# A spectral filter and a GeGLU network with their gradients: the first group starts on four row tiles, tables and tails move

## The chip, the cores and the metric

The kernel runs on one NeuronCore of one Trainium2 chip. Times are device microseconds of one execution. TensorE is called PE here, VectorE DVE, ScalarE ACT, GpSimd POOL; SP only issues DMAs.

## What is computed

Two branches work on x (2048 x 576, bf16) and B_x of the same size, and a gate mixes them; the kernel returns the mixed output and the gradients of everything but B_x. The forward part of the reference, cut:

```python
g = sigmoid((x * gate_w).sum(-1, keepdims=True))
X = rfft2(x.astype(float32)) * (w_r + 1j * w_i)
a = irfft2(X, s=(2048, 576)).astype(bfloat16)
b = (gelu(x @ w_gate) * (x @ w_up)) @ w_down      # width of the hidden layer: 4608
out = g * a + (1 - g) * b
```

The network reads the same x in the kernel. Gradients follow from `grad_out` (dO): through the FFT branch (a second transform of g*dO), and through the network: dA = dO (1-g) w_down^T, the two hidden gradients dHg and dHu, three weight gradients and dx.

## The kernel before

**Layout.** The rows are held as 16 row tiles of 128. Each row tile is turned on PE (a matmul against the identity `ident`) into `xT` and `dOT`, whose five column chunks are the even and odd columns in two halves each and a tail of 64 columns, kept twice (partitions `LO` and `HI`). `titems` (L347) makes three items of a source's four row tiles: two of 1024 columns, one for the tails; each is a PSUM tile and a copy by DVE (`VC`) or ACT (`AC`).

**The first stage** runs `NG` = 18 groups of 256 hidden columns, in each 4 steps of four row tiles, 72 steps in all (`pr` in the loop at L944 to L1027). In a step `H_mm` (L378) multiplies z = dOT w_down^T (16 matmuls of 256 columns and four tail ones) into a PSUM tile of pool `pz` (one buffer), then xy = xT [w_gate, w_up] into two tiles of pool `ph` (two buffers): four tail matmuls, then 8 of 512 columns per tile (`full`). ACT scales z by 1 - g into `da` (`H_da`), and copies and squares xy (`H_act`); DVE does three operations in `H_ew1`; ACT does two sigmoids and DVE eight products in `H_ew2`, the last of which gives dHg. In group 0 the sigmoids and products of a step are held back until `da` of the next (`held`).

From group 1 on, the weight gradients of the group before follow the xy matmuls in a step, as units of two halves (`W_units`, L468): `u_dw` (16 matmuls a half), `u_dwd` (8 a half) and the tail (8 row tiles a half, two matmuls each, that use half of the array's columns). Their PSUM tiles are in pool `pw` (two buffers, opened at group 1 in the place of `pg`), and ACT copies them out.

**The transform units** are a list of 207 slots (`fft`, L890): `u1` and `u2` of the forward transforms (column and row part), `s2` and `s1` of the filter, `z`, `ztail` and `d` of the inverse ones, some empty (`gap`). Each takes a PSUM tile by `pftile` (L541), from group 1 on always from pool `pz`, the same buffer as z, and ACT copies it out. `want(pr)` (L910) says how many slots are done by step `pr`: `FIRST` for the first eight steps, then an even share. Of the n units of a step the first goes ahead of the last four xy matmuls (`xy_full(1, fft_next)`), the others go between the halves of W units, at the places that `spots` gives in estimated microseconds `at` of the W work so far (L1001 to L1009); what is left goes to the end of the step (L1010). Then come the stores and the step's sigmoids.

**Tables.** `build_D` makes column tables, `build_R` the row tables of four row tiles, `build_B` that of the filter; integer parts are made by DVE and POOL, the sines by ACT. The sines of `build_R` and `build_B` are put on the list `tb.late` and done by `run_late`. [...]

**The head** (L862 to L884): x of all row tiles and dO of the first eight are turned, the gate is computed for all rows (80 matmuls of one column), the column tables and half of the row tables are made; then step 0 begins. dO of the other eight is turned in step 0.

**The second stage** (from L1032) reads the stored hidden arrays back by transposing DMAs and multiplies out b and dx. The change doesn't touch it. The order on every engine is the order of the program.

Of the kernel before, what the change touches and what calls it, by code (L numbers as in the profile page):

```python
# [63 lines left out]
def iotas(nc, res, unit):  # L64
    tb = Tables()
    G = nc.gpsimd
    kw = dict(allow_small_or_imprecise_dtypes=True)
    tb.lrow = unit([HF], F32, name="lrow")
# [4 lines left out]
    G.iota(tb.dcol[:, 4:5], pattern=[[0, 1]], base=512, channel_multiplier=1, **kw)  # L73
    tb.dn = res.tile([P, 5], F32, name="dn")
    nc.vector.tensor_scalar(tb.dn[:], tb.dcol[:], 1.0 / D, None, op0=ALU.mult)
# [9 lines left out]
    tb.qcol_i = res.tile([P, 1], I32, name="qcol_i")  # L85
    G.iota(tb.qcol_i[:], pattern=[[0, 1]], base=0, channel_multiplier=1)
    par_i = res.tile([P, 1], I32, name="par_i")
    nc.vector.tensor_single_scalar(par_i[:], tb.qcol_i[:], 1, op=ALU.bitwise_and)
    tb.par = res.tile([P, 2], F32, name="par_f")
    nc.vector.tensor_copy(tb.par[:, 1:2], par_i[:])  # L90
    nc.vector.tensor_scalar(tb.par[:, 0:1], tb.par[:, 1:2], -1.0, 1.0, op0=ALU.mult, op1=ALU.add)
    nc.vector.tensor_scalar(tb.kadd[:, 0, 1:2], tb.par[:, 1:2], float(S // 2), float(S // 4), op0=ALU.mult, op1=ALU.add)
    tb.halfpi = res.tile([P, 1], F32, name="halfpi")
    nc.vector.memset(tb.halfpi[:], math.pi / 2)
    tb.pi = res.tile([P, 1], F32, name="pi")
    nc.vector.memset(tb.pi[:], math.pi * EPS_SCALE)
    tb.npi = res.tile([P, 1], F32, name="npi")
    nc.vector.memset(tb.npi[:], -math.pi * EPS_SCALE)
    tb.warm = res.tile([P, 1], F32, name="warm")
    nc.scalar.activation(tb.warm[:], tb.halfpi[:], ACT.Sin)  # L100
    tb.late = []
    tb.Dt = []
    return tb
# [7 lines left out]
def build_D(nc, tb, unit, res, c0, n):  # L111

    V = nc.vector
    step = 2.0 * math.pi / D
    TS = (nc.gpsimd if c0 else V).tensor_scalar
    X = unit([n, HF], F32, name="XD")
    y = unit([n, HF], F32, name="yD")  # L120
    for c in range(n):
        TS(y[:, c, :], tb.lrow[:], tb.dn[:, c0 + c:c0 + c + 1], MAGIC, op0=ALU.mult, op1=ALU.add)
    TS(y[:], y[:], -MAGIC, -float(D), op0=ALU.add, op1=ALU.mult)
    for c in range(n):
        V.scalar_tensor_tensor(X[:, c, :], tb.lrow[:], tb.dcol[:, c0 + c:c0 + c + 1], y[:, c, :],
                               op0=ALU.mult, op1=ALU.add)
    o = unit([n, 2, HF], name="Dt")
    V.scalar_tensor_tensor(y[:], X[:], -1.0, X[:], op0=ALU.mult, op1=ALU.max)
    nc.scalar.activation(o[:, :, 0, :], y[:], ACT.Sin, bias=tb.halfpi[:], scale=-step)
    nc.scalar.activation(o[:, :, 1, :], X[:], ACT.Sin, scale=-step * EPS_SCALE)  # L130
    if c0 < 4:
        tb.Dt += [o[:, c] for c in range(n)]
        return
    tails = unit([2, 2, HF], name="Dt")
    nc.gpsimd.memset(tails[HI, :, :, :], 0.0)
    for par in range(2):
        V.tensor_scalar(tails[LO, par], o[LO, 0], tb.par[LO, par:par + 1], None, op0=ALU.mult)
    tb.Dt += [tails[:, par] for par in range(2)]
# [90 lines left out]
def kernel(  # L229
# [32 lines left out]
    gwT = res.tile([P, 5], BF16, name="gwT")  # L262
    one = res.tile([1, 1], BF16, name="one")
    nc.vector.memset(one[:], 1.0)
    nc.vector.memset(gwT[:, 4:5], 0.0)
# [7 lines left out]
    def load_w(g, part):  # L273
# [4 lines left out]
        if part == 0:  # L278
            wgu = wts[g][0]
            for w, c0 in ((B_w_gate, 0), (B_w_up, FG)):  # L280
                cols = slice(c0, c0 + FG)
                LD.dma_start(wgu[:, 0:4, cols].rearrange("p (e k) f -> p e k f", e=2),
                             w[0:512, fsl].rearrange("(k p e) f -> p e k f", e=2, p=P))
                for r in (LO, HI):
                    LD.dma_start(wgu[r, 4, cols], w[512:D, fsl])
# [11 lines left out]
    ident = res.tile([P, P], BF16, name="ident")  # L297
    make_identity(nc, ident[:])
    tb = iotas(nc, res, unit)
# [5 lines left out]

    gwr = unit([D], name="gwr")
    LD.dma_start(gwr[0:1, :], gate_w.rearrange("(o d) -> o d", o=1))
    load_x(0)
    load_do(0)
    wdn = unit([2, D], name="wdn")  # L310
    LD.dma_start(wdn[:], B_w_down[0:FG, :].rearrange("(c p) d -> p c d", p=P))
    for k in range(1, 4):
        load_x(4 * k)
    load_do(4)
    load_w(0, 0)
    load_do(8)
    load_do(12)
# [9 lines left out]
    pg = pgs.enter_context(tc.tile_pool(name="pg", bufs=1, space=PSUM))  # L327
# [8 lines left out]
    tb.Rt = []  # L336
# [3 lines left out]
    hctr = [0]  # L340

    def headps():
        hctr[0] += 1
        pool, tag = ((pg, "pg"), (ph, "xy"), (pz, "z"), (ph, "xy"))[hctr[0] % 4]
        return pool, tag

    def titems(src, dst, t0, ps, copies, n=4):  # L347

        def item(k, cs):
            def f():  # L350
                tp_ = ps(BF16).rearrange("p b (j t m) -> p b j t m", j=2, t=4)
                for j, c in enumerate(cs):
                    for tt in range(n):
                        if c < 4:
                            nc.tensor.transpose(tp_[:, 0, j, tt, :], src[:, t0 + tt, eo(c)], ident[:])
                        else:
                            for r in (LO, HI):
                                nc.tensor.transpose(tp_[r, 0, 0, tt, :], src[:, t0 + tt, 512:D], ident[:])
                copies[k](dst[:, cs[0]:cs[0] + len(cs), t0:t0 + n, :], tp_[:, 0, 0:len(cs), 0:n, :])
# [3 lines left out]
    def gate(ps):  # L363
        lps = ps()[:, 0]
        for t in range(T):
            for ci in range(5):
                nc.tensor.matmul(lps[:, t:t + 1], lhsT=xT[:, ci, t, :], rhs=gwT[:, ci:ci + 1],
                                 start=(ci == 0), stop=(ci == 4))
        nc.scalar.activation(g_bf[:], lps[:, 0:T], ACT.Sigmoid)
        V.tensor_scalar(omg_bf[:], g_bf[:], -1.0, 1.0, op0=ALU.mult, op1=ALU.add)  # L370
        V.tensor_copy(omg32[:], omg_bf[:])
        V.tensor_copy(g32[:], g_bf[:])
        V.tensor_scalar(gs32[:], g32[:], SD2, None, op0=ALU.mult)
# [4 lines left out]
    def H_mm(g, m):  # L378
# [7 lines left out]
        for t in ts:  # L386
            for ci in range(4):
                nc.tensor.matmul(zo(t), lhsT=dOT[:, ci, t, :], rhs=wdT[:, ci, :], start=(t % 4 < 2 and ci == 0), stop=False)  # L388
        for t in ts:
# [16 lines left out]
    def ewt(tag):  # L406
        return ew.tile([P, 4, FG], BF16, tag=tag, name=tag, bufs=1 if tag in ("q", "s", "om") else 2)

    def H_da(m, z):
        da = ewt("da")  # L410
# [13 lines left out]
    def H_ew1(tiles):  # L424
        xb, q, hu = tiles
        s = ewt("s")
# [13 lines left out]
    def H_ew2(g, m, tiles, s, da):  # L440
        xb, q, hu = tiles
        om = ewt("om")
# [21 lines left out]

    def wevac(out, in_):
        nc.scalar.copy(out, in_)  # L466

    def W_units(g):  # L468
# [45 lines left out]
        def tail(half):  # L514
            wps = wtile("t")
            for t in range(8 * half, 8 * half + 8):
# [3 lines left out]
            if half == 0:  # L520
                return
# [4 lines left out]
        tl_ = halves(tail, 1.0)  # L526
        w = [u_dw(k, ov, c0) for k, ov in ((1, o4v), (2, o5v)) for c0 in range(0, 4, TPB)]
        d = [u_dwd(fch, h) for fch in range(FCH) for h in range(2)]
        if g == 0:
            return [[w[0], tl_], d[:3], [d[3], w[1]], [w[2]], w[3]]  # L530
# [8 lines left out]
    fctr = [0]  # L539

    def pftile(dt=F32):  # L541
        fctr[0] += 1
        n = 512 if dt is F32 else 1024
        if pw is None and fctr[0] % 2:
            return pg.tile([P, 2, n], dt, tag="pg", name="pf")
        return pz.tile([P, 2, n], dt, tag="z", name="pf")

    def pgtile(dt=F32):
        return pg.tile([P, 2, 512 if dt is F32 else 1024], dt, tag="pg", name="pf")

    def on_pg():
        return pw is None and fctr[0] % 2

    def fwd_units(src, dst, scale, ps=pftile):
        ys = {}

        def u1(t):
            def f():
                yps = ps()
                for par, j in [(par, j) for par in range(2) for j in range(2)] + [(0, 2), (1, 2)]:  # L560
                    ci, tab = (4, 4 + par) if j == 2 else (2 * par + j, 2 * par + j)
# [10 lines left out]
        def u2(t):  # L572
            def f():
# [8 lines left out]
                n0 = 1 if on_pg() else 0  # L582
                nc.scalar.copy(ve[:, n0:2].rearrange("p o c l -> p o (c l)"), vps[:, n0:2, :2 * HF])  # L583
                v = [vps[:, 0, :2 * HF].rearrange("p (c l) -> p c l", c=2) if n0 else ve[:, 0], ve[:, 1]]
# [267 lines left out]
    def head_tile(dt=F32):  # L852
        pool, tag = headps()
        return pool.tile([P, 2, 512 if dt is F32 else 1024], dt, tag=tag, name="fx")

    VC, AC = V.tensor_copy, nc.scalar.copy

    def turn(src, dst, k, copies):
        for f in titems(src, dst, 4 * k, head_tile, copies):
            f()  # L860

    gps = head_tile()[:, 0]  # L862
    for c in range(5):
        w = gwr[0:1, eo(c)] if c < 4 else gwr[0:1, 512:D]
        r = slice(0, P) if c < 4 else HI
        nc.tensor.matmul(gps[r, c:c + 1], lhsT=w, rhs=one[:], start=True, stop=True)
    AC(gwT[:, 0:4], gps[:, 0:4])
    AC(gwT[HI, 4:5], gps[HI, 4:5])
    build_D(nc, tb, unit, res, 0, 2)
    turn(xn, xT, 0, (VC, VC, AC))  # L870
    build_D(nc, tb, unit, res, 2, 2)
    turn(dB, dOT, 0, (AC, VC, AC))
    build_D(nc, tb, unit, res, 4, 1)
    for f in titems(wdn, wts[0][1][:].rearrange("p k (c m) -> p k c m", c=2), 0, head_tile, (VC, AC, VC), n=2):
        f()
    turn(xn, xT, 1, (VC, AC, VC))
    turn(xn, xT, 2, (VC, AC, VC))
    turn(xn, xT, 3, (VC, AC, VC))
    turn(dB, dOT, 1, (AC, VC, AC))
    gate(head_tile)  # L880
    build_R(nc, tb, unit, 0)
    build_R(nc, tb, unit, 4)
    run_late(tb)
# [23 lines left out]
    FIRST = (0, 0, 0, 0, 3, 7, 11, 14)  # L907
# [36 lines left out]
    for g in range(NG):  # L944
# [3 lines left out]
        for m in range(NPR):  # L948
# [9 lines left out]
            z, xy_full = H_mm(g, m)  # L958
            tiles = [ewt(tag) for tag in ("xb", "q", "hu")]
# [308 lines left out]
```

## Time and profile before

| | us |
|---|---|
| median of three runs | 1429.37 (1429.21 to 1432.71) |
| the profiled execution, its time | 1427.83 |
| its span, first to last instruction | 1426.0 |
| first z matmul of step 0 | 19.63 |
| ... of step 4 (group 1 begins) | 53.70 |
| ... of step 5 | 73.56 |
| ... of step 8 | 118.75 |
| ... of step 71 (the last) | 950.94 |
| mean TensorE clock granted | 0.995 |

The table reads: the first group and the head take 54 us, the first stage about 963 us, the second the rest. Steps of the middle take 11.5 us without transform units and 12 to 15 with them. The profile gives for each engine its busy time, for each instruction its start and duration, and for the idle time before an instruction what ended it.

### The profile page before, as it was taken

The numbers are of one execution on the slowest core, as the hardware profiler recorded it, in microseconds if no ns is written. First come the engines' busy times: TensorE is split into PE (matmuls) and PEld (weight loads), VectorE is DVE, ScalarE is ACT, GpSimd is POOL, SyncE is SP. The second block draws the span as 40 slices with busy tenths as digits, with TensorE's granted clock in tenths as the row PEclk, the third lists the DMA queues.
The fourth block names the chain that finished last, engine by engine and source line by source line (L and its number), as shares of the span: only waits on it lengthen the run. The fifth ranks groups of instructions, "written<-read, shape, count | busy, mean of one in ns | idle before, by whom it ended". The sixth has DMA issues, their size and how long they took to land.

```text
span 1426.0 us, 28163 instructions
## 1 busy us (share of the span) xinstructions
PE 1392.6 (98%) x11431; PEld 1023.3 (72%) x11431; DVE 729.2 (51%) x1396; ACT 730.5 (51%) x1320; POOL 222.1 (16%) x418
## 2 busy tenths in 40 slices
PE   7799999999999999999999999999999999999997
PEld 5466767767766667667767767768777777777775
DVE  5776465656887788784665656551000742112100
ACT  6777677777788787877777776671000000000000
POOL 1020101122444433320100010100000100000000
PEclk9999999999999999999999999999999999999999
DMA  5073434355565655455356464759999998888772
GB/s 197 1 198 98 127 106 120 109 152 135 153 160 134 157 147 144 125 152 148 111 159 171 122 167 132 177 127 257 192 185 196 239 194 167 160 160 167 156 155 62
DMA packets 509534, 214.62 MB, mean 151 GB/s; under 512 B 311418, under 2 KB 502588, under 8 KB 509404
## 3 DMA queue, kind: packets, MB, share of 16 engines
q1 hardware_dynamic: 493724, 187.57, 56.8%
q0 software_dynamic: 13872, 24.24, 6.1%
q8 instruction: 89, 1.46, 0.4%
q10 hardware_dynamic: 1808, 1.02, 0.2%
q14 instruction: 41, 0.34, 0.1%
HBM read 41.05 MB, written 93.84 MB: 95 GB/s over the span
## 4 chain that ended last, share of the span: by engine, by line
PE 92%; ACT 3%; DVE 2%; DMA 1%; SPq 1%; issue 0%; POOL 0%; ACTq 0%; DVEq 0%; POOLq 0%
PE acc L1113 29%; PE xy L402 17%; PE wps L505 17%; PE wps L488 9%; PE z L388 9%; PE xy L395 2%; PE wps L518 2%; PE pf L562 2%; PE z L391 2%; SPq L1043 1%; DMA wd_all<-in_B_w_down_dram 1%; ACT ZT L810 1%; PE pf L833 1%; PE pf L672 1%; PE pf L761 1%; PE pf L835 1%
## 5 line engine op out<-in xcount | busy, mean ns | idle before, releaser
L1113 PEld LDWEIGHTS <-pin 128*128 128x128 bf16 x3456 | 337.9, 98 | 86.5 <-issue 0.9
L402 PE MATMUL xy<-wgu,xT 128*128 128x512 bf16 x1152 | 275.1, 384 | 0.0
L505 PEld LDWEIGHTS <-xn 128*128 128x128 bf16 x2304 | 224.9, 98 | 39.7 <-issue 1.7
L402 PEld LDWEIGHTS <-xT 128*128 128x128 bf16 x1152 | 107.4, 98 | 140.3 <-issue 34.6
L448 DVE TENSOR_TENSOR xb<-xb,s 128x1024 bf16<-128x1024 bf16 x72 | 49.8, 692 | 254.3 <-ACT s L444 254.3
L1130 ACT COPY bo<-acc 128x288 f32<-128x288 f32 x32 | 12.7, 398 | 304.8 <-PE acc L1113 304.8
L488 PE MATMUL wps<-dB,A 128*128 128x288 bf16 x1152 | 153.8, 286 | 0.0
L1113 PE MATMUL acc<-wgT,pin 128*128 128x288 bf16 x1152 | 143.9, 286 | 0.5 <-ACT dw L466 0.5
L1113 PE MATMUL acc<-wuT,pin 128*128 128x288 bf16 x1152 | 143.6, 286 | 0.2 <-DMA pin<-scr 0.2
L388 PE MATMUL z<-wdT,dOT 128*128 128x256 bf16 x1152 | 137.5, 272 | 5.7 <-ACT ve L583 1.0
L1113 PE MATMUL acc<-wd_all,pin 128*128 128x288 bf16 x1152 | 142.6, 286 | 0.0
L505 PE MATMUL wps<-dHg,xn 128*128 128x256 bf16 x1152 | 136.1, 273 | 0.8 <-DVE dHg L455 0.8
L505 PE MATMUL wps<-dHu,xn 128*128 128x256 bf16 x1152 | 136.2, 273 | 0.0
L488 PEld LDWEIGHTS <-A 128*128 128x128 bf16 x1152 | 112.0, 98 | 31.0
L511 POOL DMA_DIRECT2D out_dram<-dw x67 | 49.7, 742 | 519.0 <-ACT dw L466 518.8
L388 PEld LDWEIGHTS <-dOT 128*128 128x128 bf16 x1152 | 111.6, 98 | 25.6 <-issue 11.2
L412 ACT ACTIVATE da<-z,omg 128x256 bf16<-128x256 f32 x288 | 111.8, 470 | 3.2 <-PE z L391 2.4
L421 ACT CAST xb<-xy 128x512 bf16<-128x512 f32 x144 | 85.5, 594 | 32.1 <-PE xy L402 32.1
L1190 DVE SCALAR_TENSOR_TENSOR f32t<-gwf,dlog,b16t 128x576 f32<-128x576 f32 x16 | 13.1, 817 | 171.0 <-DMA b16t<-dxa_scr 171.0
L419 ACT ACTIVATE q<-xy 128x512 bf16<-128x512 f32 x144 | 88.2, 616 | 8.5 <-DVE om L450 3.7
L422 ACT CAST hu<-xy 128x512 bf16<-128x512 f32 x144 | 87.9, 610 | 0.0
L466 ACT CAST dw<-wps 128x512 bf16<-128x512 f32 x72 | 42.1, 585 | 87.3 <-PE wps L505 79.2
(208 smaller groups left out, 1692.4 us busy)
## 6 DMA issues: line engine op xcount, KB each, us to landing
scr<-A SPq DMA_DIRECT2D x72, 256.0 KB, 2.8
scr<-dHg SPq DMA_DIRECT2D x72, 256.0 KB, 3.2
scr<-dHu SPq DMA_DIRECT2D x72, 256.0 KB, 3.3
out_dram<-dw POOLq DMA_DIRECT2D x67, 128.0 KB, 2.5
wd_all<-in_B_w_down_dram SPq DMA_DIRECT2D x3, 1728.0 KB, 14.9
out_dram<-dwd POOLq DMA_DIRECT2D x34, 144.0 KB, 3.1
scr_p<-Vt SPq DMA_DIRECT2D x32, 145.0 KB, 3.0
wgu<-in_B_w_gate_dram SPq DMA_DIRECT2D x18, 256.0 KB, 4.0
```

What stands on the lines that cost most here:

```text
L388: nc.tensor.matmul(zo(t), lhsT=dOT[:, ci, t, :], rhs=wdT[:, ci, :], start=(t % 4 < 2 and ci == 0), stop=False)
L402: nc.tensor.matmul(xy[k][:, t % 2, :], lhsT=xT[:, ci, t, :], rhs=wgu[:, ci, :], start=False, stop=(ci == 3))
L412: nc.scalar.activation(da[:, t, :], z[:, t % 2, t // 2, :], ACT.Copy, scale=omg32[:, 4 * m + t:4 * m + t + 1])
L419: nc.scalar.activation(q[:, h, :], xy[:, :, 0:FG], ACT.Square)
L421: nc.scalar.copy(xb[:, h, :], xy[:, :, 0:FG])
L422: nc.scalar.copy(hu[:, h, :], xy[:, :, FG:2 * FG])
L448: V.tensor_tensor(xb[:], xb[:], s[:], op=ALU.mult)
L466: nc.scalar.copy(out, in_)
L488: nc.tensor.matmul(wps[:, :288], lhsT=tl(0, t)[:, fch * P:(fch + 1) * P], rhs=dB[:, t, h * 288:(h + 1) * 288], start=(t == 0), stop=(t == ...
L505: nc.tensor.matmul(wps[:, cc, :], lhsT=xn[:, t, (c0 + cc) * P:(c0 + cc + 1) * P], rhs=tl(k, t), start=(t == 0), stop=(t == T - 1))
L511: wst[0].dma_start(ov[:, c0:c0 + TPB, fsl], dw[:])
L1113: nc.tensor.matmul(acc[:, :288], lhsT=src[:, r, :], rhs=w_of(r)[:, h * 288:(h + 1) * 288], start=(first and r == 0), stop=(last and r == F ...
```

## The change

- Loads: dO of four row tiles first, then the weights' rows `wdn`, x, the group's weights, and dO and x in turn for the rest. `gate_w` and the tails of the first weights are loaded by ACT's queue.
- Head: 30 matmuls on the identity, then only four row tiles of dO and x are turned, after the weights. The tail of a row tile is turned once as part of 128 neighbouring columns, so each tile has its tail in one half and other columns in the other; the gate's vector and the column table get a zero half to match (two versions).
- Group 0: the other row tiles of dO and x are turned a step ahead, and the gate is computed per four row tiles, its small operations on ACT. `q`, `s` and `om` get tiles of their own there (pool `unit`).
- Tables: only `build_R(0)` stands in the head, `build_R(4)` and `columns_B` in step 0, the others in step 5; sines run in steps 4 and 6 ahead of the W units, whose PSUM copies go to DVE for the rest of that step.
- `FIRST` is lower by five units at step 7; with two units in a step the second is placed by `spots[0]`.
- The tail of a W group is one piece of 2.0 estimated us in place of two of 1.0; the order of group 0's W units is another; dB is scaled in two parts.

The diff, cut to its core:

```diff
     gwr = unit([D], name="gwr")
-    LD.dma_start(gwr[0:1, :], gate_w.rearrange("(o d) -> o d", o=1))
-    load_x(0)
+    nc.scalar.dma_start(gwr[0:1, :], gate_w.rearrange("(o d) -> o d", o=1))
     load_do(0)
     wdn = unit([2, D], name="wdn")
     LD.dma_start(wdn[:], B_w_down[0:FG, :].rearrange("(c p) d -> p c d", p=P))
+    load_x(0)
+    load_w(0, 0, nc.scalar)
     for k in range(1, 4):
+        load_do(4 * k)
         load_x(4 * k)
-    load_do(4)
-    load_w(0, 0)
-    load_do(8)
-    load_do(12)
+    tb = iotas(nc, res, unit)
...
-    pg = pgs.enter_context(tc.tile_pool(name="pg", bufs=1, space=PSUM))
+    pg = pgs.enter_context(tc.tile_pool(name="pg", bufs=2, space=PSUM))
...
-    def gate(ps):
-        lps = ps()[:, 0]
-        for t in range(T):
+    def gate(k):
+        lps = pgtile()
+        ts = slice(4 * k, 4 * k + 4)
+        for t in range(4 * k, 4 * k + 4):
...
-        nc.scalar.activation(g_bf[:], lps[:, 0:T], ACT.Sigmoid)
-        V.tensor_scalar(omg_bf[:], g_bf[:], -1.0, 1.0, op0=ALU.mult, op1=ALU.add)
-        V.tensor_copy(omg32[:], omg_bf[:])
...
+        nc.scalar.activation(g_bf[:, ts], lps[:, ts], ACT.Sigmoid)
+        nc.scalar.activation(omg_bf[:, ts], g_bf[:, ts], ACT.Identity, bias=1.0, scale=-1.0)
+        nc.scalar.copy(omg32[:, ts], omg_bf[:, ts])
...
-        tl_ = halves(tail, 1.0)
+        tl_ = [(2.0, tail)]
...
-            return [[w[0], tl_], d[:3], [d[3], w[1]], [w[2]], w[3]]
+            return [[w[0], tl_], [w[1], d[0]], d[1:], [w[2]], w[3]]
...
+    warm = pftile()
+    for _ in range(30):
+        nc.tensor.matmul(warm[:, 0, :P], lhsT=ident[:], rhs=ident[:], start=True, stop=True)
...
+    D0 = build_D(nc, tb, unit, 0, 2)
+    D0[0]()
+    D0[1]()
...
+    D2 = build_D(nc, tb, unit, 2, 2)
+    D2[0]()
+    D4 = build_D(nc, tb, unit, 4, 1)
+    parity = iotas_R(nc, tb, res, unit)
+    for f in titems(dB, dOT, 0, (pgtile, pgtile, phtile), (VC, AC, VC)):
         f()
-    turn(xn, xT, 1, (VC, AC, VC))
-    turn(xn, xT, 2, (VC, AC, VC))
-    turn(xn, xT, 3, (VC, AC, VC))
-    turn(dB, dOT, 1, (AC, VC, AC))
-    gate(head_tile)
+    for f in titems(wdn, wts[0][1][:].rearrange("p k (c m) -> p k c m", c=2), 0, (phtile, pgtile, pgtile), (AC, VC, VC), n=2):
+        f()
+    for f in titems(xn, xT, 0, (pgtile, pgtile, pgtile), (VC, AC, VC)):
+        f()
+    D2[1]()
+    D4[0]()
+    D4[1]()
+    parity()
+    D4[2]()
     build_R(nc, tb, unit, 0)
-    build_R(nc, tb, unit, 4)
-    run_late(tb)
...
-    FIRST = (0, 0, 0, 0, 3, 7, 11, 14)
+    FIRST = (0, 0, 0, 0, 0, 3, 5, 9)
...
+            if g == 0:
+                pgs3 = (pgtile,) * 3
+                if m < NPR - 1:
+                    t1 = 4 * m + 4
+                    cp = ((VC, VC, VC), (VC, VC, VC)) if m == 0 else ((VC, VC, AC), (AC, VC, VC))
+                    its = titems(dB, dOT, t1, pgs3, cp[0]) + titems(xn, xT, t1, pgs3, cp[1])
+                else:
+                    its = []
+                z, xy_full = H_mm(g, m, [lambda: gate(0)] if m == 0 else its[:2])
+                da = H_da(g, m, z)
+                if m > 0:
+                    for f in its[2:]:
+                        f()
+                if held:
+                    held.pop()()
+                xy = xy_full(0)
+                if m == 0:
+                    for f in its:
+                        f()
+                    build_R(nc, tb, unit, 4)
+                    columns_B(nc, tb, res)
+                    next(makeB)
+                for part in (1, 0):
+                    H_act(0, xy, tiles, part)
+                xy = xy_full(1)
                 for part in range(2):
                     H_act(1, xy, tiles, part)
...
+                if m < NPR - 1:
+                    gate(m + 1)
+                state += [H_ew1(g, tiles), da]
...
+                if pr == 4:
+                    scale_dB(12)
+                elif pr == 5:
+                    scale_dB(4)
+                    build_R(nc, tb, unit, 8)
+                    build_R(nc, tb, unit, 12)
+                elif pr == 6:
+                    next(makeB)
                 side_work(4.4)
                 at, k = 0.0, min(n, 1)
                 spots = (0.0, 1.6, 3.6) if n < 4 else (0.0, 1.0, 2.6, 4.2, 5.0, 5.0)
+                tables = pr in (4, 6)
                 for w, f in carry + hs:
-                    if k < n and at >= spots[k]:
+                    if k < n and at >= spots[k - (n == 2)]:
                         fft_next()
                         k += 1
+                    if tables and k == n:
+                        run_late(tb)
+                        wcopy[0] = VC
+                        tables = False
...
-                if pr == 6:
-                    run_late(tb)
```

## The prediction, made before the changed kernel was run

> **What bounds the kernel now.** I read the page's busy shares first, then what TensorE (PE) waits for, by stretches, then the timeline of the first 120 us, and last the places where a step's first matmul is late.
>
> ```profile
> span 1426.0 us, 28163 instructions
> PE 1392.6 (98%) x11431; PEld 1023.3 (72%) x11431; DVE 729.2 (51%) x1396; ACT 730.5 (51%) x1320; POOL 222.1 (16%) x418
> ```
>
> PE is busy all the time. A step of the FFN loop (four row tiles; "step n" is `pr` = n) takes on PE exactly the sum of its pieces: a step without extras is 6.06 us from its first z matmul to the next (29.67 to 35.73), a half of a dw unit 1.75, of a dwd unit 0.98, a u1 unit 0.75, u2 or s2 0.25, d 0.51, z unit 0.45. Step 10 runs from 146.33 to 160.10 and leaves no gap. So after about 120 us every microsecond in which PE stands is lost, and every one taken out is won. Before that, the waits of PE in the first 75 us (microseconds in all, times, the longest):
>
> ```profile
> PE xy L395 <- ACT q L419: 3.0, 2, 1.9
> PE xy L395 <- ACT hu L422: 2.8, 3, 1.1
> PE fx L355 <- DMA xn<-in_A_x_dram: 2.6, 1, 2.6
> ...
> PE wps L505 <- DVE dHg L455: 0.8, 1, 0.8
> ```
>
> ScalarE (ACT) is late there because it is one half of a loop with VectorE (DVE), whose turns are the steps of group 0 (timeline: start, duration, and in brackets the idle time before it and what ended it):
>
> ```profile
> 45.62 0.69 DVE L448 TENSOR_TENSOR xb<-xb,s 128x1024 bf16<-128x1024 bf16 x1 [1.87 <-ACT s L444]
> ...
> 54.25 0.69 DVE L448 TENSOR_TENSOR xb<-xb,s 128x1024 bf16<-128x1024 bf16 x1 [1.88 <-ACT s L444]
> ```
>
> A turn is 8.6 us: eight DVE products (4.9), ew1 (1.5), then 2.0 in which DVE waits for two sigmoids of 1.06. The last dHg of group 0 ends at 68.14, and the first dw unit waits for it. Last, the end of step 6:
>
> ```profile
> 100.76 0.41 PE L579 MATMUL pf<-Y,Rt 128*128 128x290 bf16 x2
> 102.14 1.91 PE L388 MATMUL z<-wdT,dOT 128*128 128x256 bf16 x16 [0.97 <-ACT ve L583]
> ...
> 110.09 1.04 PE L562 MATMUL pf<-Dt,xT 128*128 128x290 bf16 x6 [2.59 <-ACT da L412]
> ```
>
> Here an FFT unit was the last thing of the step. Its PSUM tile is from pool `pz` (one buffer), which the next step's z uses too, so z stands until ACT has copied it out (0.65). The 2.59 is ACT behind two table loads and three sines.
>
> [...] from 42.4 to 45.9 weights of the 512-column matmuls come every 0.43 us, else 0.21; a window so slowed costs 1.7. It happens three times (42, 59.5, 110). [...] Here the load is 1.28 and the next instruction follows 0.01 later (105.14, 106.44): I use 1.28.
>
> **The change, part by part.**
>
> (1) Start. Before, z of step 0 began at 19.63, after twelve transpose items of x, six of dO, the gate and the weights. Afterwards it needs dO tile 0 and the weights' turn, with x tile 0 ahead of it on PE. x landed at 5.08 with dO behind it; dO is now first on SP, so 4.6, and 30 warm matmuls fill PE till 5.0. Nine items then go through two single-bank slots: copies of 0.69 (1024 wide) and 0.42 (512 wide) on DVE, 1.01 on ACT. DVE is free from both angle blocks at 5.9, copies dO to 7.0 and the weights to 8.3; the last x items leave PE at 9.7. ACT has five DMA issues (0.35 to 0.7), table load and two sines till 6.5, which these cover. z at 10.0, bounds 9 and 11.5.
>
> (2) Group 0. What left the head comes back in the steps: 20 transposes per source tile (0.067 each) and 20 gate matmuls (0.54) for each of steps 1 to 3. On PE that is cheap. DVE after x: D4 0.67, parity 0.6, wait for ACT's sines to 12.1, four tail tables 1.0, build_R 1.55: 14.7; six copies of step 0 to 19.2; build_R 1.55, columns_B 1.25, ew1 1.5: 23.7 (E). In a step with transposes the sigmoids now stand on ACT behind two copies, which stand behind PE items that wait for DVE copies: after E, copy 0.69, PE 0.5, ACT 0.58 beside DVE 0.67 and PE 0.7, ACT 1.0, sigmoids 2.2, so 5.4 in place of 2.0. Products therefore start at 29.1, at +4.9+1.5+5.4 = 40.9, at +8.4 = 49.3 (no transposes in step 3) and +8.4 = 57.7; the last dHg ends at 62.6 (68.14 before). The own tiles for q, s, om take away PE's 1.9 waits but not this loop.
>
> Step 4: PE has z at about 50 and finishes xy at 57.5; then 12 matmuls and it stands 4 us till 62.7, so half clock (+1.7): 2.2 left of the dw unit, 1.7, tail 2.0. Step 5 begins at 68.5 to 69.0. FFT units in steps 4 to 7 are 0, 3, 2, 4 for 3, 4, 4, 3; what before did by then without the 3 units (1.75) would be 71.8. Gain so far 2.9.
>
> (3) Tables. Step 4's two sines and two loads fall while PE waits for dHg: nothing; without that cover 4.0. In step 6 the loads go ahead of the W units and evacuations go to DVE. Before, steps 6 and 7 lost 0.97 + 2.59 + 0.73 and a slow window 1.7: 6.0. Afterwards DVE's B product waits for ACT (1.28 + 0.7 + 0.7 + 0.4 after the unit's copy) and the first dwd evacuation stands behind it; `pw` has two buffers, so the third dwd unit waits about 3.2. Step 7 has two units at its end (0.9 + 0.9). Sum 5.0. Gain 1.0.
>
> Start of step 8: 118.75 less five units not yet done (2.75) is 116.0 against 112. **Head: -4.1**, bounds +2 and -14 (the latter if PE's waits shrink to 8 us of the 18 that I add up).
>
> (4) Tails in one stretch. Between halves of other shape PE loses 0.1 per switch; step 10 (4 units, m = 2) takes 13.77, step 8 with the same units 13.65. 0.14 in the 11 steps with a unit between the tail's halves: **-1.5**. But the spots are counted in the same microseconds (0, 1.7, 3.4, then the end at 5.4 where the second half at 4.4 was): spots 3.6 (three units) and 4.2 (four) now find no W unit any more, and the last FFT unit goes to the end of the step, right ahead of z. I worked `want` out for FIRST ending in 9: steps 10 and 14 (u2), 18 (u1), 50 and 54 (d), 58 and 62 (z); by a fifth unit also 16 (u1) and 56 (d). Price from the three cases seen: u2 at 102.14, u1 at 118.75 (117.86 due), d at 879.44 (878.49 due): 0.9, 0.9, 0.95; for z a copy of 1.01: 1.25. 2 x 0.9 + 2 x 0.9 + 3 x 0.95 + 2 x 1.25 = **+9.0**; bounds 6.5 (copy alone) and 12 (a W copy ahead of it each time). A gain is excluded: nothing else stands behind the unit.
>
> (5) `spots[k - (n == 2)]`. With two units, the second now comes straight after the four matmuls that follow the first. In step 34:
>
> ```profile
> 471.94 0.41 PE L672 MATMUL pf<-Vp,Btab 128*128 128x289 bf16 x2
> 472.19 1.03 PE L402 MATMUL xy<-wgu,xT 128*128 128x512 bf16 x4
> 473.05 1.91 PE L505 MATMUL wps<-dHg,xn 128*128 128x256 bf16 x16
> ```
> ```profile
> 472.87 1.28 ACT L677 CAST Xx<-pf 64x578 bf16<-64x578 f32 x2
> ```
>
> The first unit's tile is free at 474.15; PE is there at 473.05. Steps 26, 34, 38 begin with s2 (1.1 each), 30 and 42 with s1 (copy ends 422.91, PE at 422.40: 0.5): **+4.3**, bounds 2.5 and 5.5. Before, a half of 1.75 lay between. Waits of z on Xx and Xg (1.6 in all) shift a little: -0.5.
>
> Five units more over steps 8 to 64 are work that was only moved. Loads: an x or dO tile of 590 KB takes 1.4 at the 415 GB/s of 5 to 10 us in the table of stretches, so two of them keep well ahead of a step of 11. Phase 2 is the same code.
>
> **Sum.** Profiled execution 1427.83 (span 1426.0 and 1.8 around it): -4.1 - 1.5 + 9.0 + 4.3 - 0.5 = +7.2, so 1435.0. The median of the runs, 1429.37, lies 1.5 above it: **1436.5**.
>
> **Rivals.**
> A, not slower: the head keeps what it gets. z starts 9.6 earlier, two slow windows and the 2.59 go. For: PE's work to step 8 is only 84 us from z, and the waits that I add (4 before dHg, 3.2 in step 6) hang on my order of DVE's queue. Against: DVE's loop of group 0, in which the transposes' copies lengthen two turns. From a head gain of 11.3 on, the steady loss is paid; at 14 the time is 1426.6 (1420 to 1431). 22%.
> B, the ends of steps cost nothing since other slack takes them: 1429.37 - 4.1 - 2.0 = 1423.3. Against: steps 8 to 64 have no slack, and three such ends are seen to cost. 7%.
> C, the head gives nothing: PE goes to half clock in steps 1 and 2 too, with transposes alone for some 4 us (1.7 each), or step 6 waits longer. 1429.37 + 11.3 + 1 = 1441.7 (1439 to 1444). 14%.
> Forecast: 57%, its own 1432 to 1440.
>
> **Numbers.** Within 0.3% (4.3 us) is about what a measurement of this kernel can't tell from no change: 1425.1 to 1433.7. Forecast above that in nine of ten; A splits half within, half below; B mostly below. Slower 0.52 + 0.14 = 0.66; within 0.06 + 0.11 + 0.02 = 0.19; faster 0.15. Range 1425.5 to 1442.5: leaves out A's and B's lower parts and C's tail.
>
> **What would show it.** Right: z first at 10 +- 1.5; last dHg of group 0 near 62.6 with a PE wait of 4 us behind it; step 8 at 112 +- 3; nine steps that begin with PE waiting for ACT evacuations of FFT units, about 1 us each, and five waits of FFT units after the four matmuls. Wrong: step 8 before 105 (A), or those starts without a wait (B). A step 8 later than 116 is C.

## The result, and the profile after

The changed kernel takes 1435.42 us (median of 4 runs, 1434.88 to 1437.24), the kernel before 1429.29 in as many. The ratio is 1.0041, 95% interval 1.0022 to 1.0060: slower by some 6 us, close to the predicted 1436.5. The profiled execution took 1435.61, its span 1433.8, against 1426.0 before: +7.8 where the sum said +7.2. The median of before went up and down by some 4 us from chip to chip (1426.7 to 1430.3 in the runs below), so each kernel is compared by its ratio to the kernel before, measured beside it on the same chip.

The first line of the page and its busy shares, after:

```profile
span 1433.8 us, 28098 instructions
...
PE 1380.7 (96%) x11357; PEld 1026.5 (72%) x11430; DVE 735.9 (51%) x1403; ACT 731.4 (51%) x1324; POOL 222.6 (16%) x420
```

PE is busy for 11.9 us less than before and the span is 7.8 longer, so PE seems to stand 19.7 us more. Much of that is only missing records (11,357 matmuls against 11,430 weight loads): the page has 9.6 us of idle time before xy matmuls that waited for nothing. Where PE stands is better read from its waits. What PE waits for in the first 75 us (microseconds in all, times, the longest), after:

```profile
PE wps L525 <- DVE dHg L473: 5.8, 1, 5.8
PE pf L373 <- DVE dOT L374: 2.0, 2, 1.7
```

Of the waits of xy for `q` and `hu`, 5.8 us before, one of 0.4 is left. One wait has grown from 0.8 to 5.8: the first dw unit, for the last dHg of group 0. And the same view for 115 to 975 us, first before, where the z matmuls waited 3.5 us in all, then after:

```profile
PE z L388 <- ACT ev L839: 0.8, 1, 0.8
PE z L388 <- ACT Xg L677: 0.8, 2, 0.4
PE z L388 <- ACT Xx L677: 0.8, 2, 0.4
PE z L388 <- ACT Y L567: 0.7, 1, 0.7
PE z L388 <- ACT RT L625: 0.4, 1, 0.4
```

```profile
PE z L402 <- ACT ev L844: 3.0, 4, 0.8
PE z L402 <- ACT Vt L769: 2.4, 1, 2.4
PE z L402 <- ACT ZT L815: 2.2, 2, 1.1
PE z L402 <- ACT Y L575: 1.7, 2, 0.8
PE z L402 <- ACT ve L588: 1.5, 2, 0.7
...
PE pf L677 <- ACT Xg L682: 0.8, 1, 0.8
PE pf L677 <- ACT Xx L682: 0.8, 1, 0.8
```

All of these but one are what the prediction's parts (4) and (5) named: a copy of a transform unit by ACT (`ve`, `Y`, `ev`, `ZT` at the ends of steps, `Xg`, `Xx` between two units). The one that it did not name is the second line, a single wait of 2.4 for `Vt`.

When the first z matmul of a step starts, and the difference (after less before):

| step | before | after | difference |
|---|---|---|---|
| 0 | 19.63 | 9.74 | -9.89 |
| 4 | 53.70 | 50.28 | -3.42 |
| 5 | 73.56 | 70.73 | -2.83 |
| 8 | 118.75 | 112.43 | -6.32 (2.75 of it is work put off) |
| 26 | 364.52 | 363.81 | -0.71 |
| 33 | 454.31 | 454.91 | +0.60 |
| 34 | 466.74 | 470.17 | +3.43 |
| 50 | 671.11 | 675.80 | +4.69 |
| 65 | 879.44 | 887.26 | +7.82 |
| 71 | 950.94 | 958.76 | +7.82 |

The head wins 6.3, and steps 8 to 64 give back 14.1. After step 65 nothing changes between these two traces, the second stage included. But in two kernels of the experiments that change the head alone, the part from the start of step 71 on takes 472.8 and 476.6 us in their traces (475.1 here), so causes are read from the starts of steps rather than from whole times.

### The profile page after: what moved, and what is told of

Read it like the earlier page. It is cut to its first block, busy times and chain, and to the rows that moved or that the text cites. A ratio compares the mean times of both kernels' runs of the same rounds, so it can differ in the third digit from the quotient of the medians.

```text
span 1433.8 us, 28098 instructions
## 1 busy us (share of the span) xinstructions
PE 1380.7 (96%) x11357; PEld 1026.5 (72%) x11430; DVE 735.9 (51%) x1403; ACT 731.4 (51%) x1324; POOL 222.6 (16%) x420
## 4 chain that ended last, share of the span: by engine, by line
PE 92%; ACT 3%; DVE 2%; DMA 1%; issue 1%; SPq 0%; ACTq 0%; DVEq 0%
PE acc L1140 29%; PE wps L525 18%; PE xy L418 16%; PE z L402 9%; PE wps L508 9%; PE wps L538 2%; PE xy L411 2%; PE pf L568 2%; PE z L407 2%; PE pf L838 1%; PE pf L840 1%; PE pf L677 1%; PE pf L766 1%; PE pf L812 1%; PE pf L585 1%
## 5 line engine op out<-in xcount | busy, mean ns | idle before, releaser
L418 PE MATMUL xy<-wgu,xT 128*128 128x512 bf16 x1079 | 257.7, 381 | 10.3 <-issue 9.6
L1157 ACT COPY bo<-acc 128x288 f32<-128x288 f32 x32 | 12.8, 399 | 305.0 <-PE acc L1140 305.0
L402 PE MATMUL z<-wdT,dOT 128*128 128x256 bf16 x1152 | 137.5, 272 | 13.5 <-ACT ev L844 3.0
L430 ACT ACTIVATE da<-z,omg 128x256 bf16<-128x256 f32 x288 | 112.2, 471 | 12.0 <-PE z L407 11.9
```

Of the source, the lines that this page charges most:

```text
L418: nc.tensor.matmul(xy[k][:, t % 2, :], lhsT=xT[:, ci, t, :], rhs=wgu[:, ci, :], start=False, stop=(ci == 3))
L430: nc.scalar.activation(da[:, t, :], z[:, t % 2, t // 2, :], ACT.Copy, scale=omg32[:, 4 * m + t:4 * m + t + 1])
```

## The experiments

Ratios are to the kernel before, measured beside each kernel, with their 95% intervals. A half-clock stretch is one in which the profile shows PE's clock at 0.50; in the first 120 us of the kernel before there are three, each 3.41 long, from 42.45, 59.52 and 110.72.

**The tail in two halves again, and the spots of two-unit steps as before.** They undo parts (4) and (5) one at a time.

```diff
-        def tail():
+        def tail(half):
...
-            for t in range(T):
+            for t in range(8 * half, 8 * half + 8):
...
-        tl_ = [(2.0, tail)]
+        tl_ = halves(tail, 1.0)
```

> The changed kernel with the tail of a W group again in two halves of 1.0 (all else as changed). Theory (with the tail in one piece the last transform unit of a step has no W half after it, and the next step's z waits for ScalarE to empty the one-buffer PSUM pool): the waits of z at the starts after steps 10, 14, 18, 50, 54, 58 and 62 go (7.1 us in sum), two shape switches per such step come back (1.5): 1429.8 us, those after steps 16 and 56 stay. Rival (what is lost after step 8 comes from the five transform units that were put off, whatever the tail's form): within 1.5 us of the changed kernel's 1435.4.

Measured: 1.0015 (1.0006 to 1.0024). Steps 10, 14, 18, 50, 54, 58 and 62 went from 14.42, 14.41, 14.51, 13.56, 14.01, 14.36, 14.36 to 13.73, 13.73, 13.76, 12.88, 13.32, 13.49, 13.49: 5.2 less, net of what the halves cost (5.6 expected). So the rival falls. Their units stand between halves of W work again, and their waits are gone. But step 33's wait grew from 2.4 to 3.2, and a half-clock stretch came with it, which is why the time fell by less. That z, in PE's timeline of this kernel:

```profile
466.59 3.57 PE L402 MATMUL z<-wdT,dOT 128*128 128x256 bf16 x16 [3.21 <-ACT Vt L771]
```

The 16 matmuls take 3.57 instead of 1.91; step 34 took 15.67, in the changed kernel 13.02. So the tail in one piece costs what was said, and step 33 has another cause.

```diff
-                    if k < n and at >= spots[k - (n == 2)]:
+                    if k < n and at >= spots[k - (n == 2 and pr < 8)]:
```

> The changed kernel with the shift of the second unit's place for two units kept in the first eight steps alone; from step 8 on it is placed as before, after a W half. Theory (the second unit comes right after four matmuls, while ScalarE still holds the first unit's PSUM tile): the waits of 0.5 to 1.1 in steps 26, 30, 34, 38 and 42 go, 4.3 us in sum: 1431.1 us. Rival (the wait only goes to another place, since ScalarE's copies come late anyway): above 1434.

Measured: 1.0019 (1.0010 to 1.0028). Steps 26, 30, 38 and 42 take 12.02, from 13.03, 12.57, 13.16 and 12.58: the wait between the two units has gone, and with it the rival. Step 34 comes to 13.41, because the z after step 33's wait ran in part at half clock here too (3.31 for 16 matmuls), but 12.02 where that wait is gone (below). The five steps won 2.9 in this kernel, 4.3 where step 34 is undisturbed.

**The other way round: the kernel before with a tail in one piece.** Nothing else is changed, so the head cannot interfere.

```diff
-        def tail(half):
+        def tail():
...
-        tl_ = halves(tail, 1.0)
+        tl_ = [(2.0, tail)]
```

> The kernel before with one edit: the tail of a W group in one piece of 2.0. Theory: twelve steps (4, 10, 14, 18, 26, 34, 38, 42, 50, 54, 58, 62) now end with a transform unit ahead of z, at 0.9 to 1.5 each, 13 us, less 2.2 for the shape switches: about 1440. Rival (one stretch only saves switches): 1427.5.

Measured: 1.0071 (1.0058 to 1.0084), some +10 us, where 10.8 (13 less 2.2) was expected. The twelve steps named are the ones that got longer, each by 0.64 to 0.92. What z waits for in this kernel, 115 to 975 us:

```profile
PE z L388 <- ACT ZT L808: 4.4, 4, 1.1
PE z L388 <- ACT Vt L762: 1.9, 2, 0.9
PE z L388 <- ACT Xx L675: 1.8, 2, 1.4
```

With `Xg` (1.8), `Y` (1.7 and 1.5), `ev` (0.8) and `RT` (0.4) these are 14.3 where they were 3.5: +10.8, and less the estimated 1.5 for the shape switches 9.3; the starts of the steps say 9.8. It is the edit of the tail alone that puts the units at the ends of steps; what else the change does is not needed for it. The rival (units find another cover, 1427.5) falls.

**Step 33: the queue of DMAs, or the buffers of Vt?** In step 33 three `s1` units follow each other; each copies its result into `Vt`, which has two buffers (pool `half`), and SP stores it. Of the third, ACT's timeline in the changed kernel says

```profile
469.31 0.81 ACT L769 CAST Vt<-pf 128x580 bf16<-128x580 f32 x1 [3.33 <-DMA scr_p<-Vt]
```

ACT's copy waits for a store of an earlier `Vt`; PE's z waits for the copy, since the unit holds its PSUM buffer. SP's timeline and the table by stretches (the length, then busy time and instructions of PE, PEld, DVE, ACT and POOL, PE's clock, DMA share, GB/s) for the same microseconds:

```profile
462.16 0.59 SPq L642 DMA_DIRECT2D Vp<-scr_x  x1
...
463.39 7.11 SPq L771 DMA_DIRECT2D scr_p<-Vt  x3
```
```profile
460.00:464.00 4.00, 4.00 (x31) 2.82 (x29) 3.86 (x8) 3.78 (x9) 4.00 (x9) 1.00 0.86 220
464.00:468.00 4.00, 3.75 (x31) 2.85 (x30) 3.85 (x10) 0.90 (x2) 3.36 (x7) 1.00 0.95 247
```

The stores stand on SP behind weight loads of 512 KB and the loads of `Vp` of 578 KB, with the DMA engines 86 to 95% busy. Two explanations, and two edits. The first kernel halves the tail, takes the old spots, and has GpSimd issue the `Vp` loads, so that stores of `Vt` do not stand behind them:

```diff
-        LD.dma_start(Vp[:], s[16 * p:16 * p + 16].rearrange("(g k) t c l -> (k t c) g l", g=4))
+        ST.dma_start(Vp[:], s[16 * p:16 * p + 16].rearrange("(g k) t c l -> (k t c) g l", g=4))
```

> The changed kernel with three edits: tail in halves, second unit's place as before from step 8 on, and the loads of V (288 KB each) issued by GpSimd in place of SyncE. The third is for step 33, where z waited 2.4 us for a copy that waited for a store of Vt behind two such loads. Theory: 1435.4 - 5.6 - 4.3 - 2.5 = 1423.0 us, faster than the kernel before by what the head gained and a little more. Rival for the third edit (the 16 DMA engines are full there, whichever queue issues): 1425.5. Rival for all (the losses after step 8 don't add): above 1428.

Measured: 0.9974 (0.9963 to 0.9985). The two other edits add up (the ratio is that of the third edit's rival, 1425.5), but step 33 still takes 15.23 with a wait of 2.4 for `Vt`. ACT's timeline in this kernel:

```profile
464.01 0.81 ACT L771 CAST Vt<-pf 128x580 bf16<-128x580 f32 x1 [3.29 <-DMA scr_p<-Vt]
```

The first of the stores is issued at 457.61, and the copy that waits for it starts 6.4 later; in the changed kernel these are 463.39 and 5.9, and the median store of `Vt` lands 2.7 us after its issue. So another queue for `Vp` does not help; the DMA share is 0.97 from 459 to 463 us all the same. The weight loads stayed ahead of the stores on SP, so SP's queue is only in part excluded by this kernel. The second leaves the loads with SP and gives `Vt` a pool with more buffers:

```diff
-                Vt = half([2, 2 * HF], name="Vt")
+                Vt = unit([2, 2 * HF], name="Vt")
```

> The changed kernel with the tail in halves, the second unit's place as before from step 8 on, and the s1 units' tiles Vt taken from the pool of 18 buffers in place of the pool of two (V is loaded by SyncE again). Theory (in step 33 the third s1 unit needs a buffer of Vt whose store lies behind 512 KB of weight loads and 578 KB of V; moving V's loads to another queue changed nothing, since the DMA engines themselves are full): the wait of 2.4 us in step 33 goes, and with it the half clock that follows in some runs: step 33 at 12.4 to 12.7, time 0.3 to 0.5% below the kernel before. Rival (the pool of 18 is nearly taken up there, and the wait comes back as one for it): step 33 stays near 15.

Measured: 0.9957 (0.9944 to 0.9969). Step 33 takes 12.68 (15.26 in the changed kernel), step 34 12.02. z follows W work with no gap, where before 2.4 us lay between:

```profile
460.83 1.76 PE L508 MATMUL wps<-dB,A 128*128 128x288 bf16 x13
462.42 1.91 PE L402 MATMUL z<-wdT,dOT 128*128 128x256 bf16 x16
```

With loads and stores on SP as in the changed kernel, and a DMA share of 0.97 from 459 to 463 us here too, the wait is gone. So the two buffers are its cause. That the load of the DMA engines sets how long it lasts fits the times above, but no experiment varied that load. This kernel is faster than the kernel before.

**The head: fill the wait for dHg, shorten it, or do without the warm matmuls.** First, two transform units in step 4 (in place of none), in the kernel just shown:

```diff
-    FIRST = (0, 0, 0, 0, 0, 3, 5, 9)
+    FIRST = (0, 0, 0, 0, 2, 5, 7, 11)
```

> As the run before, with FIRST = (0, 0, 0, 0, 2, 5, 7, 11): two u1 units in step 4, where TensorE waits 5.8 us for the last dHg of group 0. Theory: that wait shrinks by their 1.5 us, and so much less is left for later steps: 1.5 us less than the run before. Rival (the units' copies delay ScalarE's chain and so the products of step 4 and what follows): no gain, or a loss of 1 us.

Measured: 0.9956 (0.9943 to 0.9970), no gain on 0.9957. The first unit needs the PSUM buffer that z holds until `da` has read it, and `da` of step 4 stands on ACT behind the sigmoids of step 3. So PE waits there, and no longer for dHg. PE's timeline:

```profile
59.84 1.61 PE L570 MATMUL pf<-Dt,xT 128*128 128x290 bf16 x6 [4.08 <-ACT da L430]
```

The wait was put to use all the same: step 4 takes 20.15 with the two units and 19.92 without, though they are 1.5 us of work and ran at half clock (1.61 and 1.66 for 0.91). From the first z to step 8 this kernel takes 101.25 against 101.51, with two units more done. The gain is lost afterwards: steps 8 to 64 take 763.40 against 762.73, with two units fewer to do. The units now meet in other steps; one new wait is z's for `ZT` after step 53 (1.10), and the rest was not followed up. The rival had the result and not the reason: the last dHg comes no later (53.7 after the first z in both).

Second, 26 matmuls of which nothing is used, in the wait, in the changed kernel:

```diff
+                    if g == 0 and k == 1 and c0 == 0 and cc == 0 and t == 12:
+                        dm = pw.tile([P, TPB, FG], F32, tag="wps", name="dm")
+                        for _ in range(26):
+                            nc.tensor.matmul(dm[:].rearrange("p a b -> p (a b)"), lhsT=ident[:], rhs=xn[:, 0, 0:512], start=True, stop=True)
```

> The changed kernel with 26 matmuls of 512 columns, whose result is not used, put into step 4 between the twelfth and the thirteenth matmul of the first dW unit, where TensorE waits 5.8 us for dHg. Theory (that wait makes the clock go to half for 3.4 us, and the 20 matmuls and part of the tail after it take 2.2 us too long): the 20 matmuls take 2.2 in place of 4.4 and step 4 is 2.2 to 2.7 us shorter: 1433. Rival (they were late for another reason, or the filling runs past dHg): step 4 the same or longer by up to 1 us.

Measured: 1.0033 (1.0021 to 1.0046); the timing alone does not separate it from 1.0041, the step does. The timelines of PE in the changed kernel, then in this one:

```profile
64.13 4.42 PE L525 MATMUL wps<-dHg,xn 128*128 128x256 bf16 x20 [5.76 <-DVE dHg L473]
```
```profile
56.70 5.78 PE L528 MATMUL dm<-xn,ident 128*128 128x512 bf16 x26
62.62 2.34 PE L529 MATMUL wps<-dHg,xn 128*128 128x256 bf16 x20
```

The same 20 matmuls take 2.34 instead of 4.42: here the wait does not only cost itself, the clock of what follows is at half (0.50 from 62.47 to 69.30 in the changed kernel, 1.00 from 60 to 70 with the fill). Step 4 takes 18.51 instead of 20.45, 1.9 less where 2.2 to 2.7 was expected (without the fill it takes 19.9 to 20.1 in four other kernels with this head).

Third, the sigmoids of a step ahead of the last four transpose items on ACT, whose copies then all fall to ACT:

```diff
-                    cp = ((VC, VC, VC), (VC, VC, VC)) if m == 0 else ((VC, VC, AC), (AC, VC, VC))
+                    cp = ((VC, VC, VC), (VC, VC, VC)) if m == 0 else ((VC, VC, AC), (AC, AC, AC))
...
+                if held:
+                    held.pop()()
...
-                if held:
-                    held.pop()()
```

> The changed kernel, where in group 0 the held sigmoids and products of a step come ahead of the last four transpose items of the next one, whose copies are then all on ScalarE. Theory (the turn of group 0 is a loop through VectorE's 8 products and ew1, ScalarE's copies and TensorE's xy; what is taken out ahead of the sigmoids comes back ahead of xy, H_act and ew1): products start 2 us after ew1, in place of 5.4, but ew1 of the next step comes as late; a turn stays at 11.5 to 12, the last dHg near 62.5 to 63.5, time within 2 us of the changed kernel. Rival (the sigmoids' place alone sets the turn): turns of 8.4, the last dHg near 57.5, 5 us faster.

Measured: 1.0084 (1.0072 to 1.0097). The products start at 27.54, 41.04, 53.72 and 62.34, so that the turns are 13.5, 12.7 and 8.6 (11.7, 9.8 and 8.6 in the changed kernel) and the last dHg ends at 67.6, 3.5 later. What PE waits for in the first 75 us of this kernel begins with

```profile
PE pf L367 <- ACT dOT L374: 5.9, 2, 3.0
```

The loop turns round: PE's transposes now wait for ACT's copies, which wait behind sigmoids. PE's clock is at half in steps 1 and 2 as well (27.74 to 31.16 and 41.39 to 44.81), which is a part of the longer turns. The rest of the loss against the changed kernel is 2.6 in steps 33 and 34 (16.26 and 14.64, step 34 in part at half clock). The rival (turns of 8.4) falls; the theory had the direction and not the size.

Fourth, one warm matmul instead of 30:

> The changed kernel with 1 in place of 30 warm matmuls at the start. Theory (the first z waits for loads, VectorE's angle blocks and the chain of copies, not for TensorE): the first 16 transposes take 1.9 in place of 1.1, z of step 0 is 0 to 0.6 us later, the time stays within 1.5 us of the changed kernel. Rival (without them the clock is at half speed through the head[...]): z of step 0 1.5 to 3 us later, the gate and the first xy at half speed, 3 us slower.

```diff
-    for _ in range(30):
+    for _ in range(1):
```

Measured: 1.0063 (1.0050 to 1.0075). PE's timeline here, then in the changed kernel:

```profile
5.18 1.89 PE L367 MATMUL pf<-ident,dB 128*128 128x128 bf16 x16 [2.70 <-DMA dB<-in_grad_out_dram]
...
11.44 2.88 PE L402 MATMUL z<-wdT,dOT 128*128 128x256 bf16 x16
```
```profile
5.14 1.07 PE L367 MATMUL pf<-ident,dB 128*128 128x128 bf16 x16
```

The 16 transposes take 1.89 instead of 1.07, z begins 1.70 later and takes 2.88 instead of 1.91; step 8 begins 2.3 later and step 71 2.1 later. The rival was right about z, and about half speed as far as the 1.89 and the 2.88 show it (the table by stretches has PE's clock at 1.00 from 10 to 15 us). By the trace the warm matmuls are worth about 2 us; the ratio alone does not separate 1.0063 from the changed kernel's 1.0041.

**All that helped, in one kernel:** halved tail, old spots from step 8 on, `Vt` in pool `unit`, and the unused matmuls.

> The edits that paid, together: tail in halves, second unit's place as before from step 8 on, Vt of s1 from the pool of 18 buffers, and the 26 unused matmuls in step 4. Theory (the gains lie in different steps and add): 1.7 us below the run with the first three, which had 0.9957 of the kernel before: 0.9945, about 1419 us. Rival (the filled clock window only moves the next half-clock window elsewhere): no better than 0.9957.

Measured: 0.9936 (0.9922 to 0.9950), 1420.39 against 1430.26 beside it: faster than both kernels, by 0.64% than the kernel before. That is a little more than the 0.9945 expected, which lies within the interval. Step 4 takes 18.00 (19.92 in the kernel without the fill), step 33 12.69. The interval meets that of the kernel without the fill (0.9944 to 0.9969), so that the fill's 1.9 rest on the step, not on the times.

## Why the prediction was right, and where it was not

**Start (1).** z of step 0 was predicted at 10.0 and began at 9.74. That rests on the 30 warm matmuls, which the working took only as a filler: with one in their place z begins at 11.44, the end of its bounds. dO landed later than the 4.6 predicted (PE waits for it until 5.18 there).

**Group 0 (2).** Predicted products at 29.1, 40.9, 49.3, 57.7; measured 28.65, 40.38, 50.18, 58.80. The turn lengthened by transposes (11.8) came out at 11.7. The third is 0.9 late, and PE's clock is why. DVE's timeline (in the brackets, what it waited for), after, and in the kernel with the halved tail, which has the same head:

```profile
50.18 0.69 DVE L466 TENSOR_TENSOR xb<-xb,s 128x1024 bf16<-128x1024 bf16 x1 [3.05 <-ACT s L462]
```
```profile
48.69 0.69 DVE L466 TENSOR_TENSOR xb<-xb,s 128x1024 bf16<-128x1024 bf16 x1 [1.87 <-ACT s L462]
```

The products before it start at 40.38 and 40.07, so the turn is 9.8 in the one and 8.6 in the other. In the changed kernel, 15 recorded xy matmuls of step 2 took 4.89 us, in part at half clock; in the other, 16 took 3.62 (the clock is shown in the last section). Over the kernels with this head, the turn is 8.6 in the two whose clock stayed full in step 2 and 8.7 to 9.8 in the six where it fell.

Half clock in step 2 was named in rival C alone; the forecast left it out, which cost it 1.2. A misreading added to that: eight products take 5.2 us in the kernel before (45.62 to 50.82) and not 4.9, so that its turns are 8.6 where the forecast reckons with 8.4. In the lengthened turn this does not show, since 5.1 lay between ew1 and the products (35.31 to 40.38) where 5.4 was reckoned. The sum up to E gives 23.5 and not 23.7; ew1 ended at 22.9. The last dHg ended at 64.08 (62.6 predicted; 62.59 in the kernel with the halved tail), and the wait for it was 5.8 (4). The half-clock stretch behind the wait was 6.83 long (62.47 to 69.30), of which PE worked 5.2, so that it cost some 2.6, half of that, where the forecast had 1.7. Step 5 began at 70.73 against 68.5 to 69.

**Tables (3).** Step 6's wait for the third dwd unit was predicted as 3.2 and is 1.88; step 7 ends with two units that wait 0.79 each (0.9 each predicted). The two table loads of step 6, ahead of the sines and ahead of the sigmoids after them, took 1.28 each (93.13 and 96.17). PE's timeline:

```profile
97.04 2.12 PE L508 MATMUL wps<-dB,A 128*128 128x288 bf16 x16 [1.88 <-DVE dwd L486]
...
112.43 0.38 PE L402 MATMUL z<-wdT,dOT 128*128 128x256 bf16 x2 [0.79 <-ACT ve L588]
```

The waits are the ones named; the size of the first was 1.3 too high, which gave back part of group 0's loss. Step 8 was predicted at 112 and began at 112.43: the head won 3.6 where 4.1 was forecast (its own figures make that 4.0, 116.0 less 112). Rival A, from a gain of 11.3, was far from it.

**Tails in one stretch (4).** The nine steps named (10, 14, 16, 18, 50, 54, 56, 58, 62) are the nine that have it anew. PE's timeline at the end of step 10:

```profile
153.12 0.42 PE L585 MATMUL pf<-Y,Rt 128*128 128x290 bf16 x2
154.28 1.91 PE L402 MATMUL z<-wdT,dOT 128*128 128x256 bf16 x16 [0.73 <-ACT ve L588]
```

The unit is the last thing of the step and z waits for its copy. Over the sum of a step's pieces that is 0.90 there, then 0.89, 1.00, 0.99, 0.90, 0.90, 0.91, 1.25, 1.25: 9.0, as predicted. Rival B falls with it: nothing else takes up such an end, and the experiment that changes the tail in the kernel before shows it in another head. The nine gaps ahead of z, of 0.7 to 1.1, are all on the one buffer of `pz`. That a second buffer would close them was not tried.

**Spots (5).** Predicted 4.3. Steps 26, 30, 34, 38 and 42 lie 1.01, 0.55, 1.00, 1.14 and 0.56 above their pieces: 4.26. The wait in step 26, after:

```profile
371.14 0.41 PE L677 MATMUL pf<-Vp,Btab 128*128 128x289 bf16 x2 [0.85 <-ACT Xg L682]
```

**What was missing.** Over steps 8 to 64 the sum said +11.3 and the trace says +11.4 (14.1 less the 2.75 put off). Two misses hide in that. The 14 steps of (4) and (5) already lost some 4.3 us over their pieces before, and the sum took out only 2.0 for them (-1.5 and -0.5): a term mis-sized by 2.3, which made the forecast too slow. Against it stands step 33, 12.43 before and 15.26 after: 2.6 more than the 12.68 that its new pieces take without the wait, a loss that no part foresaw. The step that failed there is "Five units more over steps 8 to 64 are work that was only moved": it counted the work of the units and not which units then meet in a step. With five fewer slots done, three `s1` units stand in step 33, and the two buffers of `Vt` do not hold them. That the two misses cancel is luck. Had only one of them been there, the forecast would have been off by some 2.5 us, still in its range.

The profiled sum was 0.6 us too low, and the predicted median 1.1 too high, because the 1.5 between the profiled run and the median of before was a matter of those three runs: after, the median lies 0.2 below the profiled run.

What stays open: whether and when a half-clock stretch falls in step 2, which takes 11.73 to 13.42 us in the kernels with this head, was not controlled by any experiment; a third buffer for `Vt` alone was not tried, only another pool; and the other parts of the change to the head (loads, the split gate, the tables) were not undone one at a time.

## What to carry to other kernels

Where an order of work is planned in estimated microseconds, merging two pieces moves every place that is counted in them: work out which piece now stands last in each step, and whose buffer it holds. A gain at the start is only as good as the loop that follows it: here 9.9 us at z became 2.8 at step 5, since DVE and ACT set the turns (11.7, 9.8 and 8.6) and PE's clock fell to 0.50 behind the waits (38.58 to 41.99 and 62.47 to 69.30). And when work is put off or brought forward, list which pieces meet in a step afterwards, with the buffers that they share.

## What the runs showed of the hardware

**Half clock came in multiples of 3.41 us, in step 2 in one trace and not in another.** In the changed kernel PE's clock is at half from 38.58 to 41.99 and from 62.47 to 69.30: the stretches are 3.41 and 2 x 3.41 long, and their starts lie 7 x 3.41 apart. In the kernel before, the starts of its three lie 5 x 3.41 and 15 x 3.41 apart. In the kernel with the halved tail it is at half from 59.20 to 66.03; counted back from there by 7 x 3.41, as an estimate, the same spacing gives stretches from 35.31 and 38.72. So the table can be asked for these stretches. The one ahead of step 2's xy matmuls and the one that holds them, in the changed kernel, then in the kernel with the halved tail:

```profile
35.17:38.58 3.41, 1.68 (x24) 1.43 (x25) 2.12 (x4) 2.29 (x5) 0.00 (x0) 1.00 0.45 133
38.58:41.99 3.41, 3.19 (x11) 1.21 (x10) 1.97 (x4) 1.74 (x2) 0.00 (x0) 0.50 0.00 0
```
```profile
35.31:38.72 3.41, 2.12 (x27) 1.65 (x27) 1.92 (x4) 2.32 (x3) 0.00 (x0) 1.00 0.33 99
38.72:42.13 3.41, 3.41 (x32) 1.76 (x31) 2.16 (x4) 3.07 (x6) 0.00 (x0) 1.00 0.00 0
```

PE is busy for 49% of the first stretch in the one and 62% in the other, and the clock of the next is 0.50 and 1.00. Step 2 takes 13.42 and 11.73 in them, 11.73 in one other run of the same head and 12.7 to 12.8 in five, whose clock fell at 36.2 to 37.4. In the changed kernel PE did transposes alone from 36.05 to 38.58; in the kernel before, a stretch with xy matmuls (39.04 to 42.45, busy for 1.56 of 3.41, that is 46%) was followed by 0.50 too. Whether the busy share decides, and at what share, is not shown.

A wait of 3.2 us cost 4.9 in one place: step 33's z in the kernel with the halved tail waited 3.21 and then took 3.57 instead of 1.91. And a store that came late while the DMA engines were 95% busy came no sooner when the loads beside it were issued from another queue (the DMA share was 0.97 then): the wait for `Vt` was 2.4 with either.
